# Keeping the inverse transform's exchange in SBUF, with a fixed order of stages and mixed tile widths

## The chip, the cores and the metric

One NeuronCore of a Trainium2 chip. The metric is the device time of one execution in microseconds (us). Engines: PE (TensorE; PEld is its weight load), DVE (VectorE), ACT (ScalarE), POOL (GpSimd), SP (SyncE, which here only issues DMAs). SBUF is the on-chip memory, PSUM the banks that PE writes.

## What is computed

Three stages in a row, on x of 8 x 3072 x 256 in fp32:

```
X = rfft(x, axis=1); y = irfft(X * (filt_r + 1j * filt_i))
logits = y @ w_gate; e = argmax(logits)              # one of 8 experts per token
h = relu(y @ w1[e]); m = gate * sigmoid(y @ w_output_gate)[e] * (h @ w2[e])
out = relu(m @ w_in) ** 2 @ w_out                    # 256 -> 2048 -> 256, 64-bit weights
```

There are 24576 tokens; an expert's inner width is 1024.

## The kernel before

**The Fourier stage** factors the 3072 points as 64 x 48 and runs in four groups (NG, two batch rows each), each through three kinds of step. *A* (12 per group, `steps_a`): DFT over 64 points with the twiddles, four products of 256 columns; one PSUM half is copied by ACT, the other by DVE, and the result is stored to the DRAM scratch `s1` two steps later. *B* (32 per group, two k1 at a time, `b_first`, `b_mid`, `b_second`): loads 192 KB of `s1`, DFT over 48 points (L330 or L334), two copies that swap real and imaginary rows into `q` (L336, L337 on ACT), products with the filter on DVE (L338) and POOL (L339), their sum on DVE (L347), the inverse DFT over 48 points (L355 or L358), a copy by ACT (L360), and a store to the scratch `s2` (L364). Its filter tile serves a pair of steps; `load_f` fills one of four buffers with six DMAs (L231, L239), and `dup_f` (L244) copies it to the upper half of the partitions. *C* (24 per group, two n2 at a time, `c_first`, `c_second`, `c_third`): loads 256 KB of `s2` four steps ahead (L380), the inverse DFT over 64 points (L393) into `yo`, four transposes (L402), a split into two parts, the logits (L416). Every fourth C step starts `route`, which over eight steps finds expert, weight and rank of 1024 tokens, stores the rows to `yd`, and queues eight scatters of token numbers into the lists `tab`; each C step issues at most two of them on POOL (L428).

The reads of `s1` and `s2` turn the order of the indices: that exchange is why they go through DRAM. The factors of the inverse DFT are transposes of the forward ones, made once on chip (`turn_m`).

**Order.** Each engine runs its instructions in program order. The string `order` (L537 to L562) is made by a small planner: at each place it takes the kind that is least far along (B and C offset by 1.2 and 2.4 groups) among those whose inputs have had 4 or 6 steps to reach DRAM. In its result A of one group, B of the one before and C of the one before that alternate; the last group's C steps come alone. The loads for a block's first four steps go out three steps ahead.

**The first layer** begins with `prelude` (about 23 steps, one per place of `order` from two places after the last B step, once three groups are routed; it also waits until those groups' scatters are issued): four tiles of 512 rows (KP) of the leading expert. Then come 40 wide tiles of 512 rows and 15 narrow tiles of 256 (`width`, L743), all of one expert each. Each tile takes eight steps of `up` (L829) and `down` (L845), 96 products in all, and transposes of its rows (L809). Its weights, 2 MB whatever its width, come in quarters: a quarter of the next tile is loaded while the same quarter of this tile runs (L760), and split two quarters later (L789 on ACT, L790 on DVE). `turn_x` writes the split rows with the row index outermost, so an engine's writes step by 16 bytes (L812, L813). The second layer's 64-bit weights are decoded by DVE in small pieces beside the first 35 tiles or so.

**The second layer** reads the results in tiles of 512 rows; `split_t` (L888, L889, L897) reads them with the same 16-byte step.

Of the kernel before, what the change touches and what calls it, by code (L numbers as in the profile page):

```python
# [27 lines left out]
NG = PR  # L28
# [12 lines left out]
NTILE1 = KP + NTILE_T  # L41
NTILE2 = NT // TT
YW = D + 8


def constants():
    """Arrays that depend on the shapes alone: DFT factors with their twiddles, and signs."""
# [8 lines left out]
    # two orders of k2 on the partitions (real 0:24 and 32:56, imaginary 64:88 and 96:120): lower half  # L56
    # first, or upper half first
# [16 lines left out]
    for r in (0, 55, 64, 119):  # L74
# [3 lines left out]
                          e[:, None] == np.arange(E)[None, :]], axis=1)  # L78
    f = np.float32
    return {  # L80
        "ma": np.ascontiguousarray(ma.transpose(1, 0, 2)).astype(f),
        "mb": mb.astype(f),
# [7 lines left out]
def spectral_moe_kernel(ctx: ExitStack, tc: tile.TileContext, x, filt_r, filt_i, w_gate, w_og, w1, w2,  # L90
                        w_in, w_out, c_ma, c_mb, c_mb2, c_sg, c_cum, out, dbg=None):
# [6 lines left out]
    s2 = [dram.tile([96 * N1, PK], F32, name=f"s2_{g}") for g in range(NG)]  # L98
# [7 lines left out]
    # ------------------------------------------------------------ constants on chip  # L106
# [18 lines left out]
    # tables over the 2 E + 1 runs of tiles: TT rows wide by expert, TS rows wide by expert, none left  # L125
# [6 lines left out]
    for i in range(2):  # L132
# [6 lines left out]
    # expert and start of its list  # L139
# [7 lines left out]
    # ------------------------------------------------------------ FFT  # L147
    # pools of stages A and B on the right, those of the last stage on the left
# [11 lines left out]
    NFB = 4  # L160
    fbuf = [fcon.tile([128, 2, KF, D], F32, name=f"fb{i}") for i in range(NFB)]
    map_, xp, aop, bip, qp, yp, bop = (right(fft, n, b) for n, b in (
        ("map", 6), ("xp", 3), ("aop", 3), ("bip", 6), ("qp", 3), ("yp", 3), ("bop", 4)))
# [7 lines left out]
    # gate weights, split, between zeros: (hi | lo) for v = 0, (hi | 0) for v = 1  # L171
    wgs = ccon.tile([128, 2, 2, 224], F32R, name="wgs")
    nc.vector.tensor_copy(wgs, segb[:, 0:1].unsqueeze(2).unsqueeze(3).to_broadcast([128, 2, 2, 224]))
    for v in range(2):
# [3 lines left out]
        ("mip", 6, {}), ("vtp", 6, {}), ("yop", 5, {}), ("ysp", 3, {}), ("rp", 2, {}),  # L178
        ("psA", 3, {"space": PSUM}), ("psL", 1, {"space": PSUM})))
    later = []  # L180
# [8 lines left out]
    # x: partition (r, a), free (j, d)  # L189
# [12 lines left out]
    def load_m(c, i):  # L202
        t = map_.tile([128, 8, 128], F32, name="m")
        nc.sync.dma_start(out=t, in_=c[:, i * 8:(i + 1) * 8, :])
        return t

    ma, mi = {}, {}

    def turn_m(i):
        """the inverse transform's factors: the transposes (1 / S is in mb2)"""  # L210
        t = mip.tile([128, 8, 128], F32, name="m")
        for h in range(2):
            ps = psA.tile([128, 4, 128], F32, name="p")
            for j in range(4):
                nc.tensor.transpose(ps[:, j], ma[i][:, 4 * h + j], ident)
            (nc.scalar.copy if h else nc.vector.tensor_copy)(t[:, 4 * h:4 * h + 4], ps)
        mi[i] = t
# [4 lines left out]
    # pair w of the units (k1 = 2 w + i) and the pair of units 64 - k1 share a filter tile: rows  # L222
    # k1 + 64 a at 0:24, rows 64 (a + 1) - k1 at 32:56; the last tile serves the units 63 and 32
# [24 lines left out]
    ma[0] = load_m(c_ma, 0)  # L248
# [7 lines left out]
    # stage A: DFT over n1, twiddles folded in  # L256
    def steps_a():
        for u in range(len(aunits)):
            g, i = aunits[u]
            if g == 0 and i % 2 == 0 and i // 2 + 1 < 6:  # L260
                ma[i // 2 + 1] = load_m(c_ma, i // 2 + 1)
            if g == 0 and i % 2 == 1:
                turn_m(i // 2)
# [17 lines left out]
    # stage B: DFT over n2, filter, inverse DFT over k2; two k1 at a time  # L281
# [3 lines left out]
    s2v = [s.rearrange("(m k) c -> m k c", k=N1) for s in s2]  # L285
# [56 lines left out]
    def b_mid(u):  # L342
        g, ka, kb, w, up = units[u]
        p, q = pq.pop(u)
        y = yp.tile([128, 512], F32, name="yt")
# [4 lines left out]
    def b_second(u):  # L350
        g, ka, kb, w, up = units[u]
        o = psO.tile([128, 2, D], F32, name="o")
        y = yt.pop(u)
        if not up:
            nc.tensor.matmul(o[0:96].rearrange("p k d -> p (k d)"), mb2[:, up], y)  # L355
        else:
            for k in range(2):
                nc.tensor.matmul(o[0:96, 1 - k], mb2[:, up], y[:, k * D:(k + 1) * D])  # L358
# [18 lines left out]
    def load_v(u):  # L377
        g, j = cunits[u]
# [3 lines left out]
    def c_first(u):  # L382
        g, j = cunits[u]
        if j + AC < UC:
            load_v(u + AC)
# [794 lines left out]
```

## Time and profile before

| | us |
|---|---|
| median of 3 runs (4098.66 to 4108.8) | 4105.96 |
| the profiled execution, its span | 4105.7 |

| busy | PE | DVE | ACT | POOL |
|---|---|---|---|---|
| us | 3841.4 | 2868.0 | 2082.6 | 785.2 |
| share of the span | 94% | 70% | 51% | 19% |

The span of the profiled execution is its own time to the tenth; no time lies around it. A group of instructions has its line, engine, operation, tiles (out<-in), shapes and count, then its busy time in us and the mean ns of one, then the idle time of the engine before it and who ended that. The ends of matmuls are modelled, so the rate of products is read from their starts.

### The profile page before, as it was taken

What the parts mean: (1) busy time and instruction counts of PE and PEld (TensorE: products, weight loads), DVE (VectorE), ACT (ScalarE), POOL (GpSimd) and SP (SyncE); (2) the same over time, 40 slices, a digit from 0 to 9 for tenths busy, and PEclk for the clock granted to TensorE, in tenths of its full rate; (3) what the DMA queues carried; (4) which work ended last, traced back from release to release, by engine and by line L of the source; (5) the groups of instructions that cost most, each with busy time, mean ns of one, the idle gap of its engine ahead of it and who ended that gap; (6) DMA issues with size and microseconds to landing.
All of it is one profiled execution on the core that took longest, in us unless ns stands there. A gap on an engine that the chain in (4) does not pass through costs nothing.

```text
span 4105.7 us, 71680 instructions
## 1 busy us (share of the span) xinstructions
PE 3841.4 (94%) x25828; PEld 3462.9 (84%) x25828; DVE 2868.0 (70%) x5037; ACT 2082.6 (51%) x3875; POOL 785.2 (19%) x743
## 2 busy tenths in 40 slices
PE   6887787699999999999899999999999999999998
PEld 4465555578888888889899999999999999999998
DVE  3555565368888777666677777777777777777775
ACT  3555465235554544455555555555555555555554
POOL 1344564511111111111001001010010110100101
PEclk9998889799999999999999999999999999999999
DMA  9899988334455555458400000000000000000000
GB/s 304 265 241 223 208 189 186 92 114 149 145 151 148 150 150 149 141 146 201 125 27 26 28 22 27 27 24 30 22 27 27 24 26 25 27 27 23 26 22 17
DMA packets 364071, 408.14 MB, mean 99 GB/s; under 512 B 84769, under 2 KB 308738, under 8 KB 360642
## 3 DMA queue, kind: packets, MB, share of 16 engines
q1 hardware_dynamic: 337440, 350.17, 31.2%
q0 software_dynamic: 25248, 53.15, 4.5%
q8 instruction: 203, 3.33, 0.3%
q14 instruction: 154, 1.26, 0.1%
q10 hardware_dynamic: 1026, 0.23, 0.0%
HBM read 271.61 MB, written 131.80 MB: 98 GB/s over the span
## 4 chain that ended last, share of the span: by engine, by line
PE 78%; DMA 8%; DVE 2%; ACT 2%; issue 2%; SPq 1%; POOL 1%; another core or an unknown queue 0%; ACTq 0%; POOLq 0%; DVEq 0%
PE py L957 26%; PE ph L911 16%; PE ph L829 12%; PE py L845 12%; PE px L911 7%; DMA r<-in_moe_w_dram 2%; DMA bi<-s 1%; DMA fb<-in_filt_i_dram 1%; DMA tab<-rowid,si 1%; PE p L393 1%; PE px L809 1%; DMA vt<-s 1%; ACT bh L888 1%; DMA fb<-in_filt_r_dram 1%; PE p L330 1%
## 5 line engine op out<-in xcount | busy, mean ns | idle before, releaser
L957 PE MATMUL py<-woh,hh 128*128 128x256 f32 x3072 | 859.8, 280 | 0.0
L957 PE MATMUL py<-woh,hl 128*128 128x256 f32 x3072 | 857.4, 279 | 0.4 <-DVE hl L944 0.4
L957 PE MATMUL py<-wol,hh 128*128 128x256 f32 x3072 | 854.6, 278 | 0.0
L957 PEld LDWEIGHTS py<-woh,hh 128*128 128x128 f32 x3072 | 578.2, 188 | 0.0
L957 PEld LDWEIGHTS py<-wol,hh 128*128 128x128 f32 x3072 | 578.0, 188 | 0.0
L957 PEld LDWEIGHTS py<-woh,hl 128*128 128x128 f32 x3072 | 576.5, 188 | 0.8 <-DVE hl L944 0.8
L966 POOL DMA_INDIRECT out_dram<-ou,io x192 | 207.9, 1083 | 1904.4 <-ACT C L933 1666.4
L911 PE MATMUL ph<-bh,wsh 128*128 128x256 f32 x1920 | 546.2, 284 | 24.9 <-ACT s L918 18.8
L833 ACT ACTIVATE hh<-ph 128x512 fp32r<-128x512 f32 (+1 forms) x472 | 256.0, 545 | 589.9 <-PE ph L829 498.9
L911 PE MATMUL ph<-bl,wsh 128*128 128x256 f32 x1920 | 539.0, 281 | 0.1
L911 PE MATMUL ph<-bh,wsl 128*128 128x256 f32 x1920 | 537.4, 280 | 0.0
L935 DVE SCALAR_TENSOR_TENSOR q<-C 128x1024 f32<-128x1024 f32 x384 | 468.1, 1219 | 2.3 <-ACT C L933 2.3
L944 DVE TENSOR_TENSOR hl<-q,hh 128x1024 fp32r<-128x1024 f32 x384 | 466.8, 1216 | 1.1 <-ACT hh L942 1.1
L834 DVE SCALAR_TENSOR_TENSOR hl<-ph,hh 128x512 fp32r<-128x512 f32 (+1 forms) x472 | 292.0, 621 | 222.3 <-ACT hh L833 194.7
L929 DVE TENSOR_TENSOR C<-ph,p 128x256 f32<-128x256 f32 x384 | 162.5, 423 | 401.1 <-ACT hh L942 278.2
L942 ACT CAST hh<-q 128x1024 fp32r<-128x1024 f32 x384 | 404.1, 1052 | 1.3 <-DVE q L935 1.3
L933 ACT COPY C<-ph 128x256 f32<-128x256 f32 x384 | 143.2, 373 | 506.6 <-PE ph L911 506.6
L911 PEld LDWEIGHTS ph<-bh,wsh 128*128 128x128 f32 x1920 | 360.9, 188 | 35.4 <-ACT s L918 28.3
L772 POOL DMA_INDIRECT xg<-yd,idx x190 | 200.6, 1056 | 954.1 <-DVE idx L782 906.9
L911 PEld LDWEIGHTS ph<-bl,wsh 128*128 128x128 f32 x1920 | 362.5, 189 | 0.4 <-DVE bl L889 0.4
L911 PEld LDWEIGHTS ph<-bh,wsl 128*128 128x128 f32 x1920 | 361.7, 188 | 0.0
L845 PE MATMUL py<-hh,wh 128*128 128x512 f32 (+1 forms) x944 | 356.9, 378 | 5.1 <-issue 5.1
(271 smaller groups left out, 8679.3 us busy)
## 6 DMA issues: line engine op xcount, KB each, us to landing
r<-in_moe_w_dram SPq DMA_DIRECT2D x448, 256.0 KB
yd<-yo SPq DMA_DIRECT2D x24, 1056.0 KB
xt<-in_x_dram SPq DMA_DIRECT2D x48, 512.0 KB
s<-ao SPq DMA_DIRECT2D x48, 512.0 KB
vt<-s SPq DMA_DIRECT2D x96, 256.0 KB
r<-ytd SPq DMA_DIRECT2D x48, 512.0 KB
bi<-s SPq DMA_DIRECT2D x124, 192.0 KB
s<-bo SPq DMA_DIRECT2D x124, 192.0 KB
```

The source lines that it names most:

```text
L772: nc.gpsimd.indirect_dma_start(out=xg[:, c, :], out_offset=None, in_=yd[0:(NT * GP // NG if t < KP else NT) + 1], in_offset=bass.IndirectO ...
L829: nc.tensor.matmul(ps, a[:, c, f2 * 128:(f2 + 1) * 128], b[:, c, 0:w], start=n == 0, stop=n == 5)
L833: nc.scalar.activation(hh, ps, AF.Relu)
L834: nc.vector.scalar_tensor_tensor(hl, ps, 0.0, hh.bitcast(F32), op0=ALU.max, op1=ALU.subtract)
L845: nc.tensor.matmul(Y[t][h], a[:, f % 2, h * 128:(h + 1) * 128], b, start=f == 0 and i == 0, stop=f == NF - 1 and i == 2)
L911: nc.tensor.matmul(ps, x[:, u, a], y[:, b], start=start and n == 0, stop=n == 2, skip_group_check=True)
L929: nc.vector.tensor_tensor(C[:, 3], V, p5, ALU.add)
L935: nc.vector.scalar_tensor_tensor(q, C, 0.0, C, op0=ALU.max, op1=ALU.mult)
L942: nc.scalar.copy(hh, q)
L944: nc.vector.tensor_tensor(hl, q, hh.bitcast(F32), ALU.subtract)
L957: nc.tensor.matmul(Z[t][k][:, c, :], x[:, 2 * i + k, c * 128:(c + 1) * 128], w[:, 2 * u + i, :], start=u == 0 and m in (0, 6), stop=u == N ...
L966: nc.gpsimd.indirect_dma_start(out=out, out_offset=bass.IndirectOffsetOnAxis(ap=io[:, c:c + 1], axis=0), in_=ou[:, c, :], in_offset=None)
```

## The change

- Stage B's inverse product is turned over: the data `y` are the stationary operand (four products, each 128 weight columns and 96 moving columns), so the result has the 256 channels on the partitions. ACT copies it into `big` (128 x 2 x 96 x 64 fp32, one buffer, 48 KB per partition), two neighbouring floats at a time; `k1_place` makes the two k1 of a step neighbours.
- Stage C no longer loads `s2`: `c_turn` takes 128 x 128 blocks of `big` and turns them back by four PE transposes; the PSUM tile is copied by DVE and ACT in turn. The factors of the inverse DFT come from DRAM (`c_mi`, rows in the order of `k1_place`), 512 KB per four C steps, two buffers. `turn_m`, `s2`, its stores and loads are gone.
- Buffers: filter tiles 4 to 3, `ao` 3 to 2, `q` 3 to 4 (the sum is now written over `q`), `vt` 6 to 2, `yo` 5 to 4, the split 3 to 2, `yt` of the first layer 2 to 1.
- The planner is replaced by a fixed order: B and C of one group follow each other as blocks (35 and 28 steps with their lags), with the A steps of the next group set among them.
- The 512-row tiles hold only full blocks of one expert, so there are 37 of them beside the leading four, and 21 narrow tiles; `slot` spreads the narrow ones among the wide ones. Their places in the results are as before, wide ones first.
- Columns of a wide tile are held by block (`p (c q)`), so `turn_x` and, for the first 41 tiles, `split_t` read and write contiguous runs.

```diff
-NTILE_L = (NT - KP * TT - E * TS) // TT
+NTILE_L = NT // TT - KP - E * (TT - 1) // TT
...
-    NFB = 4
+    NFB = 3
...
+    big = ccon.tile([128, 2, 2 * N2, N1], F32, name="big")
...
     def b_second(u):
-        o = psO.tile([128, 2, D], F32, name="o")
+        o = psO.tile([128, 2, 2 * N2, 2], F32, name="o")
         y = yt.pop(u)
...
-        b = bop.tile([96, 2, D], F32, name="bo")
-        nc.scalar.copy(b, o[0:96])
-
-        def store():
-            for d, at in rows(ka, kb):
-                nc.sync.dma_start(out=s2v[g][:, d, 0:D], in_=b[:, at])
-        later.append(store)
+        for k in range(2):
+            for h in range(2):
+                nc.tensor.matmul(o[:, h, :, 1 - k if up else k], y[:, k * D + h * 128:k * D + (h + 1) * 128], mb2[:, up])
+        at = min(k1_place(ka), k1_place(kb))
+        nc.scalar.copy(big[:, :, :, at:at + 2], o)
...
-    def load_v(u):
+    def c_turn(u):
         g, j = cunits[u]
+        pt = (psP if g < NG - 1 else psA).tile([128, 2, D], F32, name="p")
+        for i in range(2):
+            for h in range(2):
+                n = 2 * j + i
+                nc.tensor.transpose(pt[:, i, h * 128:(h + 1) * 128],
+                                    big[:, h, 2 * n:2 * n + 2].rearrange("p r k -> p (r k)"), ident)
         vt[u] = vtp.tile([128, 2, D], F32, name="vt")
-        nc.sync.dma_start(out=vt[u], in_=s2[g][j * 256:(j + 1) * 256, 0:D].rearrange("(j q) c -> q j c", j=2))
+        (nc.vector.tensor_copy if u % 2 else nc.scalar.copy)(vt[u], pt)
 
     def c_first(u):
-        if j + AC < UC:
-            load_v(u + AC)
+        if j % 4 == 0 and j + 4 < UC:
+            load_m(mi, c_mi, mip, 6 * g + j // 4 + 1)
...
+    LAGC = 4
+
+    def steps_c():
+        for g in range(NG):
+            in_g = lambda u: g * UC <= u < (g + 1) * UC
+            for u in range(g * UC, (g + 1) * UC + LAGC):
+                scatter(2)
+                if in_g(u):
+                    c_turn(u)
+                if in_g(u - 1):
+                    c_first(u - 1)
+                if in_g(u - 4):
+                    c_third(u - 4)
+                if in_g(u - 2):
+                    c_second(u - 2)
+                yield
+
+    order = "a" * UA
     for g in range(NG):
+        next_a = lambda: "a" if g + 1 < NG and order.count("a") < (g + 2) * UA else ""
+        if g == 0:
+            order += "aaaa"
+        ahead.setdefault(len(order) - 3, []).extend(lambda u=g * UB + i: load_b(u) for i in range(AB))
+        for i in range(UB + LAG):
+            order += "b"
+            if i in ((10, 18, 26), (5, 11, 17, 23, 29))[g > 0]:
+                order += next_a()
+        ahead.setdefault(len(order) - 8, []).extend(lambda i=6 * g + i: load_m(mi, c_mi, mip, i) for i in range(1))
+        order += next_a()
+        for i in range(UC + LAGC):
+            order += "c"
+            if i % 3 == 2:
+                order += next_a()
+        order += "--"
...
-    width = [TT if t < KP + NTILE_L else TS for t in range(NTILE1)]
+    NS = NTILE_T - NTILE_L
+    slot, k = [], 0
+    for i in range(NTILE_L):
+        slot.append(i)
+        while (k + 1) * NTILE_L <= (i + 1) * NS:
+            slot.append(NTILE_L + k)
+            k += 1
+    width = [TT] * KP + [TT if i < NTILE_L else TS for i in slot]
...
+        by = "p (c q) -> p c q" if w == TT else "p (q c) -> p c q"
+        hv = xh[:, h, 0:w].rearrange(by, c=n)
+        lv = xl[:, h, 0:w].rearrange(by, c=n)
```

## Rows read from the trace of the kernel before

**Rows 1.** Busy time by stage: stretch, length, busy (instructions), PEclk, DMA share, GB/s.

```profile
0.00:760.00 760.00, 576.26 (x2432) 408.76 (x2432) 413.09 (x908) 382.62 (x720) 330.57 (x314) 0.89 0.88 226
900.00:1600.00 700.00, 700.00 (x3157) 570.46 (x3156) 562.32 (x1103) 350.32 (x491) 123.82 (x122) 1.00 0.51 150
1650.00:1800.00 150.00, 150.00 (x676) 122.21 (x675) 89.51 (x128) 74.50 (x105) 22.15 (x22) 1.00 0.48 135
1817.00:2012.00 195.00, 183.25 (x1491) 179.36 (x1490) 133.05 (x259) 115.66 (x235) 33.19 (x26) 0.99 0.77 197
2015.00:4105.70 2090.70, 2047.82 (x17280) 2036.04 (x17280) 1551.17 (x2352) 1084.84 (x2208) 207.87 (x192) 0.99 0.08 25
```

**Rows 2.** DMA of 0 to 760 us: packets, and the loads of `s2`.

```profile
DMA packets 142715, 171.65 MB, mean 226 GB/s; under 512 B 20882, under 2 KB 128371, under 8 KB 139973
...
vt<-s SPq DMA_DIRECT2D x96, 256.0 KB
```

**Rows 3.** The chain that ended last, Fourier stage: start us, us, what.

```profile
308.17 1.73 PE p L272 x8
...
388.05 4.11 DMA fb<-in_filt_r_dram
...
440.77 10.96 DMA fb<-in_filt_i_dram
```

**Rows 4.** Groups of instructions by line and shape, 0 to 760 us.

```profile
L339 POOL TENSOR_TENSOR q<-q,fb 128x512 f32<-128x512 f32 x128 | 163.7, 1281 | 336.8 <-ACT q L337 120.6 <-DMA s<-ao 77.3 <-DVE fb L244 30.3
L428 POOL DMA_INDIRECT tab<-rowid,si x157 | 160.1, 1020 | 90.6 <-issue 30.2 <-DMA tab<-rowid,si 26.3 <-DVE si L497 16.2
...
L347 DVE SCALAR_TENSOR_TENSOR yt<-q,sg,p 128x512 f32<-128x512 f32 x124 | 92.2, 744 | 3.9 <-POOL q L339 1.8
L338 DVE TENSOR_TENSOR p<-p,fb 128x512 f32<-128x512 f32 x128 | 88.3, 690 | 25.8 <-ACT q L337 24.5 <-PE p L442 0.8
...
L360 ACT COPY bo<-o 96x512 f32<-96x512 f32 x128 | 74.5, 582 | 26.4 <-DMA s<-bo 13.1 <-PE o L355 7.3 <-PE o L358 2.2
...
L336 ACT COPY q<-p 64x512 f32<-64x512 f32 x128 | 73.9, 578 | 133.2 <-PE p L330 68.6 <-PE p L334 49.6 <-issue 5.0
...
L244 DVE COPY fb<-fb 64x1024 f32<-64x1024 f32 x68 | 54.9, 808 | 186.5 <-DMA fb<-in_filt_i_dram 63.5 <-DMA fb<-in_filt_r_dram 42.5 <-DMA s<-bo 35.9
```

**Rows 5.** Groups of instructions by line and shape, 880 to 1795 us.

```profile
L812 ACT CAST xh<-px 128x512 fp32r<-128x512 f32 x80 | 85.7, 1071 | 0.0
...
L850 ACT COPY yt<-py 128x512 f32<-128x512 f32 x78 | 41.9, 594 | 0.0
```

**Rows 6.** Instructions in order of time among the last C steps: start, us, engine.

```profile
690.47 1.13 PE L393 MATMUL p<-vt,m 128*128 128x256 f32 x4 [0.35 <-DVE carry L496]
...
691.81 0.46 PEld L402 LDWEIGHTS p<-ident,yo 128*128 128x128 f32 x4
...
692.24 0.73 PEld L393 LDWEIGHTS p<-vt,m 128*128 128x128 f32 x4
...
707.37 1.13 PE L393 MATMUL p<-vt,m 128*128 128x256 f32 x4 [0.66 <-ACT cn L469]
...
762.93 1.91 PE L393 MATMUL p<-vt,m 128*128 128x256 f32 x4
```

**Rows 7.** Filter loads of L239 on SP: count, ns min/median/max, first and last start.

```profile
L239 SPq DMA_DIRECT2D fb<-in_filt_i_dram x136: 297/356/1653, 23.1 to 647.1; - x136
```

**Rows 8.** The first B product's weight loads, same columns.

```profile
L330 PEld LDWEIGHTS p<-bi,mb x128: 186/190/338, 66.2 to 646.4; 96*128 96x128 f32 x128
```

**Rows 9.** The chain that ended last, the first products of two wide tiles.

```profile
1510.93 1.39 PE py L845 x6
...
1534.01 1.39 PE py L845 x6
```

**Rows 10.** Waits in 1817 to 2012 us: total us, times, longest.

```profile
ACT wh L789 <- DMA r<-in_moe_w_dram: 30.5, 21, 3.5
```

**Rows 11.** Busy time late in the narrow tiles, columns as in rows 1.

```profile
1986.00:1999.00 13.00, 13.00 (x112) 13.00 (x111) 10.06 (x19) 8.19 (x18) 1.62 (x1) 1.00 0.77 208
```

More of the change, by code (lines that the diff above doesn't have):

```diff
@@ L78, in constants @@
                           e[:, None] == np.arange(E)[None, :]], axis=1)
+    rows = np.argsort([k1_place(k) for k in range(N1)])
     f = np.float32
@@ L200, in load_x, with load_m @@
         xt[u] = t
[L202 to L205, printed above, removed]
     ma, mi = {}, {}
[L209 to L217, printed above, removed]
+    def load_m(at, c, pool, i):
+        at[i] = pool.tile([128, 8, 128], F32, name="m")
+        nc.sync.dma_start(out=at[i], in_=c[:, i % 6 * 8:(i % 6 + 1) * 8, :])
     filt = (filt_r, filt_i)
@@ L260, in steps_a @@
             if g == 0 and i % 2 == 0 and i // 2 + 1 < 6:
-                ma[i // 2 + 1] = load_m(c_ma, i // 2 + 1)
-            if g == 0 and i % 2 == 1:
-                turn_m(i // 2)
+                load_m(ma, c_ma, map_, i // 2 + 1)
             if u + 2 < len(aunits):
@@ L507, in steps_b @@
     def steps_b():
[L508 to L516 removed]
+        for g in range(NG):
+            for u in range(g * UB, (g + 1) * UB + LAG):
+                if u < (g + 1) * UB:
+                    b_first(u)
+                if g * UB <= u - 1 < (g + 1) * UB:
+                    b_mid(u - 1)
+                if u - LAG >= g * UB:
+                    b_second(u - LAG)
+                yield
     def advance():
@@ L542, in spectral_moe_kernel @@
-    at = {k: [] for k in "abc"}
-    order = ""
-    def ready(k):
-        n = len(at[k])
-        if n >= NG * size[k]:
-            return False
-        if k == "a":
-            return True
-        b = "ab"["bc".index(k)]
-        m = (n // size[k] + 1) * size[b] + lag[b]
-        return len(at[b]) >= m and at[b][m - 1] + (W0 if n == 0 and k == "b" else WAIT) < len(order)
-    while any(len(at[k]) < NG * size[k] + lag[k] for k in "abc"):
-        best = min((k for k in "abc" if ready(k)), default=None,
-                   key=lambda k: len(at[k]) / size[k] + {"a": 0, "b": 1.2, "c": 2.4}[k])
-        if best is None or 0 <= len(at["b"]) - NG * UB < LAG:
-            best = next((k for k in "abc" if NG * size[k] <= len(at[k]) < NG * size[k] + lag[k]), "-")
-        if best != "-":
-            at[best].append(len(order))
-        order += best
@@ L563, in spectral_moe_kernel @@
-    PF = 3
+        for g in range(NG):
+            in_g = lambda u: g * UC <= u < (g + 1) * UC
[9 more added lines that the diff above has]
+                    c_second(u - 2)
+                yield
+    order = "a" * UA
     ahead = {}
@@ L565, in spectral_moe_kernel @@
     for g in range(NG):
-        ahead.setdefault(at["b"][g * UB] - PF, []).extend(lambda u=g * UB + i: load_b(u) for i in range(AB))
-        ahead.setdefault(at["c"][g * UC] - PF, []).extend(lambda u=g * UC + i: load_v(u) for i in range(AC))
+        next_a = lambda: "a" if g + 1 < NG and order.count("a") < (g + 2) * UA else ""
[6 more added lines that the diff above has]
+                order += next_a()
@@ L884, in split_t @@
         bh, bl = (pl["bp"].tile([128, 7, 256], F32R, name=n) for n in ("bh", "bl"))
-        rv = [[r[:, j].rearrange("p (q c) -> p c q", c=4)[:, 2 * k:2 * k + 2] for k in range(2)] for j in range(2)]
+        by = "p (c q) -> p c q" if t < NWIDE else "p (q c) -> p c q"
+        rv = [[r[:, j].rearrange(by, c=4)[:, 2 * k:2 * k + 2] for k in range(2)] for j in range(2)]
         blk = lambda a: a.rearrange("p (c q) -> p c q", c=2)
```

58 lines of the change are left out of this document (15 added, 43 removed).

## The prediction

> **What bounds the kernel now.** I read the busy time by stage first, since each stage has a limit of its own [rows 1]. The second layer (2015 us to the end) keeps PE busy for 2048 of 2091 us, and the wide tiles of the first layer for all of 900 to 1600 us; neither is limited by anything but TensorE. Two stretches are not. In the Fourier stage, 0 to 760 us, PE, DVE, ACT and POOL are busy 576, 413, 383 and 331 us, the DMA engines 0.88 of the time, and the granted clock averages 0.89. In the narrow tiles, 1817 to 2012 us, PE idles 12 of 195 us.
>
> For the Fourier stage I then read its DMA traffic [rows 2]: 171.65 MB in 142,715 packets, so most packets are 1 KB, and 226 GB/s. The s2 exchange is 96 loads of 256 KB and as many bytes stored: 50 MB, about 49,000 packets of 1 KB. The chain of waits there names loads of the filter tile that took 4.11 to 10.96 us [rows 3]. So transfers hold this stage, and the change takes traffic from them. The question is what limits next.
>
> **Part 1, the exchange.** Busy DMA time is 0.88 x 760 = 669 us, or 4.7 ns a packet. Without s2 231 us of that go; the factors loaded again by each group (4 x 6 x 512 KB in 4 KB packets, about 3,100 packets) cost 15 us by packets or 49 us by bytes. Some 453 to 487 us stay, which no longer fill a stage of 700 us, so engine steps decide. I price one step of each kind.
>
> *A B step.* DVE: 0.69 for L338, 0.744 for L347, and half of 0.808 for the filter copy L244: 1.84 us [rows 4]. ACT: two copies into q, 0.578 each, and the copy out of o, now 384 columns instead of 512. It was 0.582; by columns it would be 0.44. It now writes pairs of floats 256 bytes apart. The nearest row for a scattered write is L812, stride 16 bytes: 1071 against 594 ns for the contiguous L850 [rows 5], so at most 384 x 2.09 ns = 0.80. ACT is 1.60 to 1.96; I take the middle. The Trainium skill (SBUF — State Buffer, in its section on the DMA port swizzle) says that each access that leaves a 16-byte line pays; the trace agrees for L812, and by it, paying on every second element, an estimate is 0.62, which changes no sum here because DVE leads. PE: the first product is half of an A step's four products of 256 columns (1.73 us [rows 3]), 0.87. The second becomes four products with 128 weight columns and 96 moving ones, each two passes. Four single-pass transposes of 128 columns follow each other in 0.43 us (691.81 to 692.24 [rows 6]), 0.107 each; eight such passes are 0.86 if the weight load sets the pace, 0.64 if the 96 columns do. I take 0.86, in place of 0.87 now: no gain. The Trainium skill (TensorE: Matmul & The Clock Gate, LDWEIGHTS) puts a weight load at columns / 1.2 ns whatever the moving side has, 107 ns here; the row agrees, and this rule speaks against narrow moving operands: by it the products cost 0.86, by the streamed columns 0.64, and over 128 steps the two differ by 28 us of PE time, though not of a step that DVE leads.
>
> So the floor of a B step is DVE's 1.84. One loop is longer. With three filter buffers instead of four, the load for pair w + 2 goes into the buffer that the previous step's POOL product still reads. From that step's first product: ACT 1.16, POOL 1.28 and hand-overs, 2.65 us; six issues on SP at 0.36 and a little between, some 2.4 [rows 7]; landing L; copy 0.81; less 1.2 because the product four steps on needs it only after its own matmul. Four steps must cover 4.66 + L, so a step is at least 1.17 + L / 4. L was 4.11 to 10.96 on the old queue; with DMA share near 0.75 I take the short end, 4.6, hence **2.3 us**. Bounds: 1.84 and, at 10.96, 3.9.
>
> *A C step.* Where C steps ran alone, seven took 707.37 - 690.47 = 16.9 us, 2.41 each with their routing [rows 6]. The change adds four transposes (0.43 on PE) and an eviction shared by ACT and DVE. I take 2.41 + 0.43 = **2.84**; below, 2.41 if the transposes fill idle PE time; above, 3.5 if a whole 0.69 eviction lands on the chain as well. Removing the vt load hides nothing else.
>
> *A steps* inside other blocks: PE 1.73 among C steps, which PE limits; about 1.0 among B steps, where an eviction like L338's 0.69 falls on DVE. *Changing blocks:* B's last step drains through 0.87, 1.16, 1.28, 0.74, 0.86, 0.6, and C fills through 0.43, 0.6, 0.87, 0.6, 0.43, 0.6: 9 us per group, which the old mixed order covered.
>
> *Queues.* SP loses 128 stores and 96 loads, gains 24 loads. The scatters (two per C step, 1.02 us each plus 0.3 between, L428 [rows 4]) now crowd on POOL: 2.6 of 2.84 us. A backlog would hold the next block's POOL product; no scatter is issued in B steps, and I book nothing because four C steps in each block issue none, with a bound of 5 us per group. Two ao buffers instead of three in the opening: 4 us (0 to 8). Dropping the 48 transposes of turn_m gains nothing there, as the opening waits for transfers. The smaller vt, yo and yt pools cost nothing as long as their cover holds: vt is filled a step ahead by PE; a yo tile lives some 18 C steps counting its store's landing, against 16 that four buffers give when that store is late, so up to 2 steps in each chunk of four are at stake, 24 x 5.7 us at worst, and none if SP issues the store as soon as its route is done, which its queue, lightened by 220 transfers, allows; yt's store has a whole tile to land.
>
> Sum to the last C product: opening 66 (the first B product now starts at 66.2 [rows 8]) + 4; B 128 x 2.3 = 294; C 96 x 2.84 = 273; A steps 13 x 1.0 + 19 x 1.73 = 46; four block changes 36: **719 us**. It now ends at 762.93 + 1.91 = 764.8 [rows 6]. Gain 46 us. The first layer starts right behind, as now: its prelude takes some 23 steps and starts with the last C block, which has 28.
>
> **Part 2, narrow tiles among wide.** A wide tile takes 1534.01 - 1510.93 = 23.08 us [rows 9], a narrow one 195 / 15 = 13.0 [rows 1], and over the 15 ACT waits 30.5 us for weights [rows 10]. The last 13 us without such a wait hold 112 products and transposes [rows 11], 0.116 each; a narrow tile has 100, so 11.6 us at PE's pace. Before: 44 x 23.08 + 195 = 1210.5. After, 41 wide and 21 narrow at 11.6: 1190, 20 less. But DVE is 8.9 us per narrow tile, and the decoding of the second layer's weights adds (562.3 / 700 - 89.5 / 150) x 23.08 = 4.8 us per tile [rows 1], 13.7 in all against 11.6. Decoding covers the first 34 tiles or so, about 11 of them narrow: 0 to 23 us back, I take 12. Net **-8** (-20 to +3).
>
> **Part 3, blocked columns.** xh and xl go from 1.07 to about 0.6 us on engines that wait for PE anyway: nothing, except at the head of the second layer, where the splits stand alone: -1.5.
>
> The profiled execution took 4105.7 us, the median is 4105.96, so no correction: 4105.7 - 46 - 8 - 1.5 = **4050**.
>
> **Rivals.** *The steps reach their floors* (B 1.84, C 2.41, part 2 full): 128 x 0.46 + 96 x 0.43 + 12 = 112 us more, 3938. For it: DMA share falls far below 0.88. Against: nothing in [rows 2] or the page shows B steps at one engine's floor. Halfway is 3994. Chance 0.14.
>
> *The clock takes half.* The mean grant is 0.89 [rows 1], which is 22% of the time at the lower of its two levels, 1.2 GHz. In a B step PE then needs 2 x 1.73 = 3.5 us, 1.2 over the step; over 22% of the B steps that is 34 us, over 40%, 61. That gives 4084 to 4111: little or no change. Chance 0.2. For it: B blocks now stand alone and PE is the only engine with a slower level. Against: C blocks become dense.
>
> *The filter buffer holds B.* If L stays at 7.5, midway in the old range, a step is 3.0 and the time 4050 + 128 x 0.7 = 4140, slower than before. It decides against the change from L = 6.5 (step 2.8). For it: loads of 24 rows queue behind x and s1 transfers and six issues share SP with the rest. Against: 30% less traffic. Chance 0.15.
>
> *It does not do what it says* (transfers still at 0.88, engines waiting as now): part 2 alone is left, 4095. Chance 0.03.
>
> **Numbers.** The forecast, 4005 to 4080, has the remaining 0.48. Faster by over 0.3% (12 us, about what a measurement tells from no change) means under 4093.6: 0.48 + 0.14 + 0.08 of the clock case = 0.70; within: the rest of it, 0.12, and the last rival, 0.15; slower: the filter case, 0.15. The range leaves out the lowest part of the floor case and the worst of the filter case: 3975 to 4125.
>
> **What would show it.** Right: no transfers of s2, DMA share under 0.75 up to 720 us; first B product near 70; B products 2.2 to 2.5 us apart in the last group's B block and C products 2.7 to 3.0 apart; last C product near 719; 0.86 us for the four products of L355's successor; the copy into big between 0.44 and 0.80; no weight waits in the first layer, ending some 55 us earlier than 2012. Wrong: waits of L244 for filter loads over 2 us in each pair, a granted clock below 0.85 in B blocks, POOL products late behind scatters, or narrow tiles at 13 us or more with PE behind hl.

## The result and the profile after

The changed kernel takes **4048.9 us** (median of 4 runs, 4045.9 to 4062.6) against 4103.65 (4098.66 to 4108.8) for the kernel before on the same chip: ratio 0.9866, 95% interval 0.9842 to 0.9891. The prediction said 4050, faster. The number came out right by luck, because most of its terms are not: on this chip the stage that was to give 46 us gave 10, and a part costed at 1.5 us gave 31, the most of all.

One thing is needed to read the figures below. The chips differ: two of them ran the kernel before in 4104 and 4107 us, the three that ran all experiments but the last in 4137 (4136.6 to 4136.9). Each ratio is to the kernel before on the same chip; experiments are compared with the changed kernel as c0_after ran it on a chip of the second kind. A profile shows one run, for c0_after the slowest of its four (4049.8 us, median 4039.4) and for e5 and e7 the fastest (4024.7 and 4007.9), so differences between two profiles carry some 10 us that the medians do not have.

Busy time by stage of the changed kernel, columns as in [rows 1]:

```profile
0.00:760.00 760.00, 645.62 (x3477) 516.54 (x3477) 448.39 (x974) 400.87 (x771) 340.87 (x332) 0.89 0.65 178
900.00:1600.00 700.00, 690.49 (x3693) 585.57 (x3692) 562.89 (x1205) 349.25 (x584) 119.51 (x118) 1.00 0.59 165
1650.00:1800.00 150.00, 150.00 (x817) 128.80 (x816) 91.61 (x153) 76.24 (x128) 29.47 (x26) 1.00 0.55 159
1990.00:4048.00 2058.00, 2033.86 (x17280) 2029.29 (x17280) 1499.44 (x2352) 1052.88 (x2208) 207.99 (x192) 1.00 0.08 25
```

The DMA share of the Fourier stage fell from 0.88 to 0.65, as the change promises. The DMA view of the same 760 us answers to [rows 2]; no load of `s2` is left in it:

```profile
DMA packets 94101, 135.01 MB, mean 178 GB/s; under 512 B 18113, under 2 KB 76450, under 8 KB 91346
```

Three lines by shape, 0 to 800 us, answer to [rows 4]. The copy into `big` took 0.493 us, between the bounds 0.44 and 0.80, and waits for filter loads fell from 106 us to 26:

```profile
L354 ACT COPY big<-o 128x384 f32<-128x384 f32 x128 | 63.1, 493 | 29.4 <-PE o L352 21.2 <-issue 5.7
L243 DVE COPY fb<-fb 64x1024 f32<-64x1024 f32 x68 | 49.3, 725 | 27.8 <-DMA fb<-in_filt_i_dram 15.1 <-DMA fb<-in_filt_r_dram 10.7 <-issue 0.2
L335 POOL TENSOR_TENSOR q<-q,fb 128x512 f32<-128x512 f32 x128 | 164.0, 1283 | 204.7 <-ACT q L333 169.6 <-DMA fb<-in_filt_i_dram 9.7 <-DMA fb<-in_filt_r_dram 8.0
```

So transfers hold this stage far less than before. Yet its last C product starts at 753.7 us instead of 764.2, where 719 was forecast. These are all C products, before and then after (ns min/median/max, first and last start):

```profile
L393 PE MATMUL p<-vt,m x384: 377/379/797, 202.0 to 764.2; 128*128 128x256 f32 x192
L389 PE MATMUL p<-vt,m x384: 379/379/634, 157.7 to 753.7; 128*128 128x256 f32 x192
```

From the traces, by stage (starts of products):

| us | before | after | predicted change | measured change |
|---|---|---|---|---|
| first B product | 66.6 | 66.1 | +4 | 0 |
| last C product | 764.2 | 753.7 | -46 | -10 |
| from there to the end of the first layer | 1248.3 | 1232.2 | -8 | -16 |
| from there to the end (second layer) | 2093.2 | 2062.4 | -1.5 | -31 |

### The profile page after: what moved, and what is told of

Read it like the earlier page. It is cut to its first block, busy times and chain, and to the rows that moved or that the text cites. A ratio compares the mean times of both kernels' runs of the same rounds, so it can differ in the third digit from the quotient of the medians.

```text
span 4048.3 us, 74500 instructions
## 1 busy us (share of the span) xinstructions
PE 3881.3 (96%) x27092; PEld 3562.3 (88%) x27092; DVE 2817.7 (70%) x5126; ACT 2040.8 (50%) x3965; POOL 776.2 (19%) x743
## 3 DMA queue, kind: packets, MB, share of 16 engines
q1 hardware_dynamic: 297600, 318.71, 27.6%
## 4 chain that ended last, share of the span: by engine, by line
PE 78%; DVE 2%; ACT 1%; DMA 1%; issue 1%; another core or an unknown queue 0%; SPq 0%; POOL 0%; POOLq 0%; ACTq 0%; DVEq 0%
PE py L958 26%; PE ph L912 17%; PE ph L829 13%; PE py L845 12%; PE px L912 7%; PE px L807 1%; DVE wl L788 1%; PE p L389 1%; DVE hl L834 0%; DMA raw<-in_moe_w_in_dram 0%; PE o L352 0%; PE p L398 0%; DMA out_dram<-ou,io 0%; PE lt L412 0%
## 5 line engine op out<-in xcount | busy, mean ns | idle before, releaser
L912 PEld LDWEIGHTS ph<-bh,wsh 128*128 128x128 f32 x1920 | 360.1, 188 | 12.4 <-ACT bh L889 5.1
L845 PE MATMUL py<-hh,wh 128*128 128x512 f32 (+1 forms) x992 | 365.0, 368 | 0.0
L829 PE MATMUL ph<-xh,wh 128*128 128x512 f32 (+1 forms) x992 | 356.5, 359 | 7.6 <-DVE hl L834 6.9
```

The costliest lines, as they stand in the source:

```text
L829: nc.tensor.matmul(ps, a[:, c, f2 * 128:(f2 + 1) * 128], b[:, c, 0:w], start=n == 0, stop=n == 5)
L845: nc.tensor.matmul(Y[t][h], a[:, f % 2, h * 128:(h + 1) * 128], b, start=f == 0 and i == 0, stop=f == NF - 1 and i == 2)
L912: nc.tensor.matmul(ps, x[:, u, a], y[:, b], start=start and n == 0, stop=n == 2, skip_group_check=True)
```

## The experiments

### Which part gives what: e1, e2, e3

e1 takes part 3 out: `turn_x` and `split_t` keep the 16-byte step of the kernel before.

```diff
-        by = "p (c q) -> p c q" if w == TT else "p (q c) -> p c q"
+        by = "p (q c) -> p c q"
...
-        by = "p (c q) -> p c q" if t < NWIDE else "p (q c) -> p c q"
+        by = "p (q c) -> p c q"
```

> The changed kernel with the columns of wide tiles held as before, so that the splits of both layers step by 16 bytes again. Prediction: the blocked columns are worth 1.5 us, all at the head of the second layer, so about 4050. Theory from the two traces: each tile of the second layer began with a wait of PE for ACT, which the 0.65 us copies of the split delayed; the second layer took 2091 us before and 2062 after, so it should take about 2090 again, the total 4075 to 4085, with the waits of the up product for ACT's first copy back at 47 us. Rival: the 28 us come from another place (the second layer's start, its stores), and then the second layer stays at 2062 to 2066. The first layer should lose 0 to 10 us, since DVE is short of time in its narrow tiles.

Measured: 4074.1 us (4068.8 to 4082.7), ratio 0.9848 (0.9815 to 0.9882); the second layer takes 2093.8 us, as before the change, against 2064.8 in c0_after. What went is seen in the waits of PE in the second layer (us in total, times, longest). The kernel before:

```profile
PEld ph L911 <- ACT s L918: 28.3, 47, 0.8
PE ph L911 <- ACT s L918: 18.8, 47, 0.6
```

The changed kernel:

```profile
PEld ph L912 <- ACT s L919: 4.0, 7, 0.6
PE ph L912 <- ACT s L919: 2.6, 7, 0.4
```

And e1:

```profile
PEld ph L912 <- ACT s L919: 26.8, 47, 0.6
PE ph L912 <- ACT s L919: 17.4, 47, 0.4
```

There are 48 tiles, so the wait stood at every change of tile. ACT in order of time at one of them, in the kernel before, shows what is late:

```profile
2173.84 1.79 ACT L888 CAST bh<-r 128x256 fp32r<-128x256 f32 x3
2175.52 0.38 ACT L918 COPY s<-ph 128x256 f32<-128x256 f32 x1
```

Three casts of the next tile's rows stand ahead of the copy `s` that PE needs. With single floats 16 bytes apart one takes 668 ns, contiguous 446 ns (the kernel before, then the changed one):

```profile
L888 ACT CAST bh<-r 128x256 fp32r<-128x256 f32 x144 | 85.9, 668 | 3.8 <-DMA idsc<-idx 3.8
```

```profile
L889 ACT CAST bh<-r 128x256 fp32r<-128x256 f32 x144 | 54.5, 446 | 4.0 <-DMA idsc<-idx 4.0
```

The wait rows show 19 us of the 31; the pace shows all of it. In the same 200 us in the middle of the layer, the kernel before and the changed one (columns as in [rows 1]):

```profile
2100.00:2300.00 200.00, 198.26 (x1683) 197.46 (x1682) 148.58 (x224) 104.48 (x216) 21.01 (x19) 1.00 0.08 24
```

```profile
2100.00:2300.00 200.00, 200.00 (x1707) 199.91 (x1706) 147.54 (x235) 103.04 (x218) 16.86 (x16) 1.00 0.08 25
```

24 products more in 200 us are 1.4%, or 29 us over the layer, at the same granted clock.

e2 keeps the changed kernel's tiles but puts the narrow ones last; e3 keeps part 1 alone (the old widths, order and column layout).

```diff
+    slot = list(range(NTILE_T))
```

> The changed kernel with its 21 narrow tiles after the 37 wide ones. Prediction: mixing is worth 8 us net (20 at best, less what DVE loses while it decodes), so 4056. Theory from the traces: in the changed kernel PE is idle only some 10 us among the mixed tiles, and 21 narrow ones in a row would cost 13.0 us each instead of 11.6 to 12.2, so 18 to 29 us more, 4066 to 4078, with waits of the weight split for its load of some 40 us in the narrow tiles. Rival: DVE's crowding takes back all that mixing gives, and the total stays within 5 us of 4048.

```diff
-NTILE_L = NT // TT - KP - E * (TT - 1) // TT
+NTILE_L = (NT - KP * TT - E * TS) // TT
...
+    slot = list(range(NTILE_T))
...
+        by = "p (q c) -> p c q"
```

> Only the Fourier stage of the change; both layers' tiles, their number, order and columns as before. Prediction: 46 us less than before, 4060. Theory from the traces: the last C product ended 10 us earlier and the first layer began 30 us earlier, so 10 to 30 us less than before, 4076 to 4096, with the second layer at 2090 again and the last C product near 754. Rival: the stage gains nothing by itself (less than 5 us).

Measured: e2 4060.4 us (ratio 0.9817, 0.9787 to 0.9848), e3 4068.3 (0.9838, 0.9806 to 0.987). From the last C product to the end of the first layer, e2 takes 1249.1 us and c0_after 1231.5: mixing the same tiles is worth 17.6 us (21 in the medians). But e3, with the old 44 wide and 15 narrow tiles, the narrow ones last, takes 1236.3, and e1, with the new tiles mixed and the old layout, 1234.6. The new cut has six narrow tiles more and three wide ones less; it takes back nearly all that mixing brings. Such times have some play: in the profiles that leave the first layer as it is in the changed kernel (c0_after, e4, e5, e6, e10, e11, e12) it takes 1220.6 to 1233.2 us. On chips of this kind part 1 alone gives 69 us (4136.9 to 4068.3), part 3 another 35 (4074.1 to 4039.4), and part 2 nothing that the runs can tell (4068.3 to 4074.1, ranges overlapping). The parts were not taken one by one on a chip of the first kind, where all together give 55 us instead of 97.

### What holds a B step: e4, e10, e6

The prediction had a loop through three filter buffers. e4 gives a fourth; e10 does the same on top of e5 (below).

```diff
-    NFB = 3
+    NFB = 4
```

> The changed kernel with four filter buffers instead of three. Prediction: the loop through the filter buffer sets the B step at 2.3 us, above the floor of 1.84; then a fourth buffer should bring B steps to 1.84 to 2.0 and the total down by 35 to 55 us. Theory from the trace: DVE and POOL waited only some 45 us for filter loads in 128 steps, and the waits for the copy out of o and for ACT are longer, so B steps stay at 2.1 or more and the total falls by less than 15 us.

> e5 with four filter buffers instead of three. If the loop through three filter buffers set the B step, as the prediction had it, B steps fall by 0.2 us or more each and this is 20 us or more faster than e5. If they do not set it (e4 had the same B steps as the first profile), it is within 8 us of e5, by what the first filter loads of a block come earlier.

Measured: e4 4036.6 us (ratio 0.9749, 0.9715 to 0.9783), c0_after's ratio being 0.9758 (0.9739 to 0.9776); e10 4034.0 (0.9743, 0.9717 to 0.9768), e5's being 0.9736. The fourth buffer does nothing that the runs can tell, and the B steps stay: 2.41, 2.73, 2.75 and 2.47 us in e4's four blocks, 2.51, 2.88, 2.78 and 2.39 in c0_after's (from the first product of a block to that of its last step, divided by the 31 steps between). On average that is 2.59 in e4, and 2.53 to 2.64 in c0_after, e1, e2, e3 and e7, whose Fourier stage is the same. The filter loop is not what holds them.

e6 takes one PSUM buffer from `p` and gives it to `o`.

```diff
-    psP = right(fft, "psP", 3, space=PSUM)
-    psO = right(fft, "psO", 1, space=PSUM)
+    psP = right(fft, "psP", 2, space=PSUM)
+    psO = right(fft, "psO", 2, space=PSUM)
```

> Two PSUM buffers for o and two for p, instead of one and three. Theory (in the B block that stands alone, the loop product, copy, product through the one o buffer, 0.9 us of TensorE wait in every second step, holds a step at 1.97 us): steps of the last group's B block fall toward DVE's 1.84, at most 4 us, and up to 15 us over all blocks. Rival (the pipe of two p buffers becomes the limit, since p waits for two ACT copies and a DVE pass): B steps of 2.6 us and more, 15 to 60 us slower.

Measured: 4308.8 us (4304.8 to 4316.2), ratio 1.0407 (1.0387 to 1.0427), 269 us above c0_after; the rival's sign, and far beyond its size. Instructions of e6 in order of time (start, us, engine, what, idle before it):

```profile
606.72 1.10 PE L326 MATMUL p<-bi,mb 96*128 96x512 f32 x2 [2.00 <-issue]
...
607.85 0.58 ACT L332 COPY q<-p 64x512 f32<-64x512 f32 x1 [2.23 <-PE p L326]
608.44 0.58 ACT L333 COPY q<-p 64x512 f32<-64x512 f32 x1
...
609.05 0.70 DVE L334 TENSOR_TENSOR p<-p,fb 128x512 f32<-128x512 f32 x1 [2.44 <-ACT q L333]
...
609.66 0.74 DVE L343 SCALAR_TENSOR_TENSOR q<-q,sg,p 128x512 f32<-128x512 f32 x1
...
610.81 1.10 PE L330 MATMUL p<-bi,mb 96*128 96x256 f32 x4 [2.13 <-DVE q L343]
```

The order on DVE closes a loop: L343 of step u, which frees p(u), stands behind L334 of step u + 1, which waits for both ACT copies of p(u + 1). With two buffers the first product of u + 2 waits for p(u). One turn is the product, 1.10, two copies, 1.17, L334, 0.70, L343, 0.74, and hand-overs: 610.81 - 606.72 = 4.09 us, and each turn is one step. The changed kernel has three buffers, and two steps in each turn. Its DVE alone, in the last group's B block:

```profile
608.26 0.70 DVE L334 TENSOR_TENSOR p<-p,fb 128x512 f32<-128x512 f32 x1 [1.27 <-ACT q L333]
608.99 0.75 DVE L343 SCALAR_TENSOR_TENSOR q<-q,sg,p 128x512 f32<-128x512 f32 x1
610.02 0.70 DVE L334 TENSOR_TENSOR p<-p,fb 128x512 f32<-128x512 f32 x1 [0.28 <-ACT q L333]
610.63 0.74 DVE L343 SCALAR_TENSOR_TENSOR q<-q,sg,p 128x512 f32<-128x512 f32 x1
611.40 0.69 DVE L243 COPY fb<-fb 64x1024 f32<-64x1024 f32 x1
612.21 0.70 DVE L334 TENSOR_TENSOR p<-p,fb 128x512 f32<-128x512 f32 x1
```

612.21 - 608.26 = 3.95 us for two steps, 1.98 each: about the same turn. So `p` is a limit that binds at once when a buffer goes. The steps of the whole stage fit this: between the starts of the inverse products (L352) of two steps that both run at the full clock the median is 3.96 us in e6, 1.98 in the changed kernel, and 1.99 in c0_after, e3 and e4. DVE's 1.84 lies just below, so a fourth buffer could bring little by itself; it was not tried. The Trainium skill (Perfetto Trace Analysis, Identifying Performance Opportunities) says that the same gap coming back on the engine that should be saturated can mean too few buffers for the next tile; here the trace agrees, with 2.00 and 2.13 us of idle PE ahead of the two products above and, over whole B blocks, steps that go from 2.4-2.9 to 4.7-5.1 us. Part of that is the clock: where e6's steps run at the lower of its two levels they take 4.90 us, and in its B blocks the granted clock is 0.50 to 0.70, in c0_after's 0.81 to 0.88.

### What the changes of block cost: e5, e11, e12

In the changed kernel 18.5, 15.9 and 21.3 us pass between the last transposes of a C block and the first product of the next B block. PE in order of time at the first of these, the last `c_turn` and the first B product:

```profile
219.04 0.60 PE L373 MATMUL p<-ident,big 128*128 128x128 f32 x4
...
237.58 3.78 PE L326 MATMUL p<-bi,mb 96*128 96x512 f32 x4 [4.47 <-DMA bi<-s]
```

e5 puts the first four B steps among the last four C steps and issues their loads five C steps earlier.

```diff
-        ahead.setdefault(len(order) - 3, []).extend(lambda u=g * UB + i: load_b(u) for i in range(AB))
-        for i in range(UB + LAG):
+        if g == 0:
+            ahead.setdefault(len(order) - 3, []).extend(lambda u=g * UB + i: load_b(u) for i in range(AB))
+        for i in range(4 if g else 0, UB + LAG):
...
-        order += "--"
+            if g + 1 < NG:
+                if i == UC - 5:
+                    ahead.setdefault(len(order), []).extend(lambda u=(g + 1) * UB + i: load_b(u) for i in range(AB))
+                if i >= UC:
+                    order += "b"
+        if g + 1 == NG:
+            order += "--"
```

> The changed kernel itself again, on the chip of the next runs. Theory: what the first profile showed repeats: B steps of 2.0 to 2.6 us, C steps of 2.7 to 2.9, and between the last block of a C stage and the first product of the next B block 16 to 21 us. Last C product 740 to 754 us, first layer ends 1232 us (within 4) after that, second layer 2062 (within 3). If the last group's C block (3.7 us a step in the first profile) was a chance collision, it is near 3.0 here; if it belongs to the kernel, it is 3.5 or more again.

> The first four B steps of groups 1 to 3 stand among the last four (draining) C steps of the group before, and their loads are issued five C steps earlier; nothing else moves. Theory (the changes between blocks cost about 25 us a group, most of it in C to B, because the B pipe fills only when C has drained and its loads start late): C to B falls from 16-21 us to about 6-10, three times: 25 to 40 us less to the last C product, and 25 to 40 us less in all. Rival (DMA sets the stage: what is saved at a change comes back as waits for bi and fb in the B block): less than 10 us, with longer B steps.

Measured: c0_after 4039.4 us (4037.3 to 4049.8), ratio 0.9758; e5 4029.6 (4024.7 to 4030.0), ratio 0.9736 (0.9718 to 0.9754), 10 us less. The same two lines of e5:

```profile
216.71 0.60 PE L373 MATMUL p<-ident,big 128*128 128x128 f32 x4
...
221.81 1.02 PE L326 MATMUL p<-bi,mb 96*128 96x512 f32 x2
```

The gap is 5.1 us, and by the first and last products of the blocks the three gaps together are 29 us shorter than in c0_after. But of the B blocks behind them two are 9 and 12 us longer (89.7 and 82.6 us from the first to the last product of L326 against 81.0 and 70.6), and the last C product comes only 14 us earlier. Even these 14 us are not shown to be e5's: e3 and e7, whose Fourier stage is c0_after's, have it at 735.3 and 737.6 us, as early as e5. What stands is the 10 us in the medians, and e12 against e11 (below), the same edit again, gives 10 us too. Both readings were half right.

What the early steps run into is on POOL, whose first products come 12.4, 13.5 and 15.2 us after PE's in e5. POOL in order of time in c0_after, where the same is seen and PE's first B product of this block starts at 235.12:

```profile
237.57 0.95 POOL L424 DMA_INDIRECT tab<-rowid,si  x1 [4.12 <-DMA tab<-rowid,si]
...
243.37 0.95 POOL L424 DMA_INDIRECT tab<-rowid,si  x1 [0.68 <-DMA tab<-rowid,si]
248.82 0.95 POOL L424 DMA_INDIRECT tab<-rowid,si  x1 [4.50 <-DMA tab<-rowid,si]
...
251.06 3.71 POOL L335 TENSOR_TENSOR q<-q,fb 128x512 f32<-128x512 f32 x3
```

The scatters go into four tables in turn, so each waits for the landing of the one four before it (6.6 us in the median here, up to 9.7), and POOL's first product comes 16 us after PE's. PE then stands still:

```profile
253.29 2.07 PE L326 MATMUL p<-bi,mb 96*128 96x512 f32 x2 [11.92 <-DVE q L343]
```

The same happens ahead of the other two blocks (430.4 after 415.8, 604.5 after 593.4). e11 moves scatters out of the C blocks into the B blocks that follow, with two buffers more for the token numbers `si`; e12 is e5 and e11 together.

```diff
-        si = rp.tile([128, TC], I32, name="si", bufs=4)
+        si = rp.tile([128, TC], I32, name="si", bufs=6)
...
+                if g and u >= g * UB + 4 and u % 3 and (g + 1 < NG or len(scat) > 20):
+                    scatter(1)
...
-                scatter(2)
+                scatter(1 if g + 1 < NG else 2)
```

> The scatters of the routing are spread: one per C step instead of two in the first three groups, and the rest two in every three B steps of the next group (the last B block leaves the same 20 to the last C block as before). Theory (in c0_after GpSimd works off a backlog of scatters, each waiting up to 4.5 us for the landing of the one four before it into the same table, and reaches its first product of the B block 11 to 15 us after TensorE's first one, in three groups; PE and ACT stand behind it): the first GpSimd product follows within 4 us, the waits of the scatters for a table fall from 118 us to under 50, and the last C product comes 20 to 35 us earlier than in c0_after; time 20 to 35 us below it (ratio 0.967 to 0.971). Rival (the backlog is covered, since B has to wait for its loads at the start anyway): under 8 us.

> e5 and e11 together. Theory: e5 gave back in the B blocks what it won at the changes because its early B steps stood behind the scatters; with these gone the two add up, 40 to 55 us below c0_after (ratio 0.962 to 0.966). Rival (both take away the same wait at the change of blocks): the same as e11 within 8 us.

Measured: e11 4071.4 us (4070.1 to 4075.3), ratio 0.9844 (0.9823 to 0.9866), 32 us slower than c0_after; e12 4061.0 (0.9817, 0.9795 to 0.9838). Both forecasts fell. POOL in e11, where PE's first product starts at 231.4:

```profile
234.72 1.26 POOL L335 TENSOR_TENSOR q<-q,fb 128x512 f32<-128x512 f32 x1 [10.28 <-ACT q L333]
...
243.27 1.26 POOL L335 TENSOR_TENSOR q<-q,fb 128x512 f32<-128x512 f32 x1 [3.33 <-DVE fb L243]
247.94 1.27 POOL L335 TENSOR_TENSOR q<-q,fb 128x512 f32<-128x512 f32 x1 [3.41 <-issue]
249.37 1.01 POOL L424 DMA_INDIRECT tab<-rowid,si  x1 [0.16 <-DVE q L343]
```

The first product does come 3.3 us after PE's, and the scatters wait 70 us for tables instead of 118. But the block is 93 us long instead of 84 (L326), the last C product comes at 781.1 us, 29 us later than in c0_after, and DVE's waits for filter loads in 66 to 760 us rise from 33 to 78 us: a scatter, 1.01 us and 0.3 between, now stands beside two of three POOL products of 1.27. That is 2.6 us in such a step and 2.1 on average, in steps of 2.4 to 2.9, so POOL has little slack, and by these waits the filter buffers that its products read come free late. The backlog's stall is real; spreading it over the B steps costs more than it frees. A cheaper way, more tables or smaller stores beside the scatters, was not tried.

### What decoding costs the narrow tiles: e7

The second layer's weights are decoded on DVE in all tiles of the first layer; e7 does it in the wide ones alone.

```diff
-        if f not in (1, 5) and dec:
+        if f not in (1, 5) and dec and width[t] == TT:
```

> Weights of the second layer are decoded in the wide tiles alone, no longer in the narrow ones. Theory (the prediction's: VectorE has 13.7 us of work in an 11.6 us narrow tile while it decodes, 12 us in all): the first layer after the last C product takes 1220 to 1227 us instead of 1231.5. Rival (TensorE idles only some 10 us in the whole mixed stretch, so VectorE's queue hides nearly all of it): 1229 to 1233, no change in the time. If the decoding then ends too late, the head of the second layer grows from its 2064.8.

Measured: 4015.9 us (4007.9 to 4023.3), ratio 0.9713 (0.969 to 0.9735), 24 us below c0_after; from the last C product the first layer takes 1205.3 us instead of 1231.5, twice the theory's estimate and 15 us below the lowest of the unchanged ones (1220.6). Windows of c0_after:

```profile
900.00:1200.00 300.00, 290.23 (x1558) 245.44 (x1556) 242.66 (x549) 148.53 (x249) 49.21 (x52) 0.99 0.60 161
1200.00:1500.00 300.00, 297.52 (x1570) 251.49 (x1569) 249.65 (x528) 148.19 (x247) 48.84 (x49) 1.00 0.62 168
```

The same of e7:

```profile
900.00:1200.00 300.00, 300.00 (x1587) 255.66 (x1587) 232.25 (x480) 152.65 (x254) 55.20 (x48) 1.00 0.59 163
1200.00:1500.00 300.00, 300.00 (x1631) 257.80 (x1630) 230.45 (x464) 153.19 (x256) 59.80 (x52) 1.00 0.60 166
```

PE idles 12 us in these 600 in c0_after and not at all in e7, and e7 does 3218 products and transposes there instead of 3128, 2.9% more. The idle time alone does not show that, since a product that follows a stall counts as busy. In c0_after decoding itself waits, too, and VectorE's queue with it (900 to 1600 us, c0_after and then e7):

```profile
DVE ea L646 <- DMA raw<-in_moe_w_in_dram: 17.1, 4, 5.4
```

```profile
DVE ea L646 <- DMA raw<-in_moe_w_in_dram: 4.3, 2, 2.4
```

The second layer starts no later for it (2063.3 us long).

### A faster version: e9

e5 and e7 together.

> e5 (first four B steps among the draining C steps) and e7 (decoding in wide tiles alone) together; scatters as in the changed kernel. Theory (the two work in different stages and add up): e7's 23.6 us and e5's 9.9 us below c0_after's 4039.4, so 4006 us, ratio 0.967 to 0.970; last C product 8 to 20 us before that of c0_after, first layer 1202 to 1208 us after it, second layer 2062 to 2066. Rival (a Fourier stage that ends earlier only makes the first layer wait for its gates and gathers): the same as e7 alone, 4016 (ratio 0.971).

Measured: 4025.8 us (4023.2 to 4031.0), ratio **0.9800 (0.9786 to 0.9813)**, on a chip of the first kind, where the changed kernel has 0.9866 (0.9842 to 0.9891): faster than both kernels, by 23 us in the medians than the changed one. The forecast was a ratio of 0.967 to 0.970, from chips of the second kind, so it neither met this nor can be tested by it; e7 alone was not run on a chip of the first kind, so what e5 adds to it there is not shown. The second layer takes 2063.4 us; the first, from the last C product, 1214.0 instead of 1232.2. The last C product is at 751.9: of the Fourier stage's gain nothing is left there. The last group's C block starts at 659.9, only 3 us earlier than in the changed kernel (663.1), and takes 86.3 us. It takes 84.9 in the changed kernel's profile on the first kind of chip and 67 to 72 in the seven profiles of c0_after, e1 to e5, and e7 on the second kind, where the prelude of the first layer runs beside it as well. Why it takes longer on the first kind is open.

## Why the prediction was right in sum and wrong in its parts

The sum met the measured time by luck. The Fourier stage was given 36 us too much, the second layer 29 and the first 8 too little, and these errors cancel.

**The exchange** was to save 46 us to the last C product and saved 10 in the profile. By the starts of products in the changed kernel:

- *B blocks.* 302.5 us over the four blocks, from the first product of each to that of its last step; predicted 124 x 2.3 + 13 A steps = 298. The size was right by luck and the cause wrong: the step "one loop is longer", through the filter buffers, does not hold (e4, e10). I had not counted the three buffers of `p`, whose turn (e6) gives 1.98 us, the median step at the full clock. Against that the sum left out the lower clock level: 18 of the 128 steps run at it, and such a step takes 3.42 us (below), some 26 us in all by an estimate of 18 x (3.42 - 1.98). The A steps and the starts of the blocks have the rest. The granted clock is 0.85 to 0.90 in these blocks.
- *C steps.* Without the A steps among them (4, 6 and 6 at 1.73 us) the first three blocks run at 2.42, 2.37 and 2.39 us, against 2.84 predicted: the four transposes and their eviction cost nothing, the lower bound. The last block, at 3.68 in this profile (3.05 in c0_after's), takes back 19 of the 31 us so gained.
- *Changing blocks* was the term that failed. Nine us per group were priced as one drain and one fill; the seven changes take 46 us from B to C and 56 from C to B, some 43 more than the 36 booked for them and the 23 that the A, B and C steps among them cost at the predicted prices. The routing's tail, loads of `bi` that start late (4.47 us above) and the scatters lie there. The scatters I had seen, bounded at 5 us per group and booked at nothing; they cost PE up to 11.9 us in one stall in c0_after, while in this profile POOL's first products come 3 to 8 us behind PE's.
- *The opening, the smaller pools and the queues* cost nothing, as said: the first B product is at 66.1 us.

The inverse products of four B steps of the last group, and the granted clock (the last figure but two) beside the first and the last of them:

```profile
600.01 1.86 PE L352 MATMUL o<-mb,q 128*128 128x96 f32 x8
603.43 1.86 PE L352 MATMUL o<-mb,q 128*128 128x96 f32 x8
...
608.79 1.13 PE L352 MATMUL o<-mb,q 128*128 128x96 f32 x8
...
610.76 1.03 PE L352 MATMUL o<-mb,q 128*128 128x96 f32 x8
```

```profile
599.00:602.00 3.00, 3.00 (x12) 2.73 (x12) 2.97 (x11) 1.25 (x3) 0.40 (x1) 0.50 0.70 226
610.50:612.00 1.50, 1.50 (x11) 1.29 (x11) 1.47 (x3) 0.99 (x3) 0.84 (x1) 1.00 0.39 84
```

**Narrow among wide** was to give 8 us. Mixing gives 17.6 over the same tiles in a row, but decoding takes back 26 (e7) instead of the 12 that I took, outside the range of 0 to 23. What is left of part 2 is e1 against e3: 1.7 us less in the first layer and 6 us more in the medians, neither clear of the play. Of the 16 us by which the first layer is shorter, 12 belong to part 1, as far as profiles on two kinds of chip can tell: e3 has them with the old tiles (1236.3 against 1248.3). That fits the first product of the layer, which now stands 11 to 16 us before the last C product instead of 4 behind it.

**Blocked columns** were costed at 1.5 us with the words "engines that wait for PE anyway". They gave 31. The page has PE busy for all but 43 us of the second layer [rows 1], and I took that for the end of the matter; the view of waits would have shown 47 of them, one per tile, on the engine that bounds the stage.

**The copy into `big`**: 0.493 us for 384 columns is 1.28 ns a column, against 2.09 for `xh` at 16-byte steps [rows 5]. The Trainium skill's rule on 16-byte lines (SBUF — State Buffer, in its section on the DMA port swizzle) made an estimate of 0.62. By the measurement, pairs of floats 256 bytes apart cost only 0.05 us over the 0.44 by columns. The estimate used half of the rule: the same sentence asks for at least two hits per line for full bandwidth, which pairs have and single floats have not. The casts of part 3 agree with it, `xh` falling from 1071 to 586 ns.

**The rivals.** The clock took no half, 0.89 over the stage before and after, but its lower level costs the B blocks some 26 us, near the 34 that this rival named. The filter loads were not late: DVE waited 26 us for them in all. The steps reached a floor in C and not in B. The price of the last rival was a slip, 4105.7 - 8 being 4098 and not 4095; it changes no chance.

## What to carry to other kernels

A wait that comes once in every tile on the engine that bounds the stage is money, however short: multiply it by its count before costing an edit at nothing. To find what holds a pipelined step, go round every ring of buffers, PSUM's too, and count how many steps share one turn of it. When mixed stages become blocks, price each change of block from the in-order queues: what is still queued on each engine when the next block's first instruction comes.

## What the hardware showed beside that

The same 297,600 packets of the main queue took 27.6% of 16 engines' span on the first chip and 29.5% on c0_after's: 1117 and 1194 us. The kernel before, at a DMA share of 0.88, differs by 33 us between such chips, but it was profiled on one of them only, so no trace shows where. The changed kernel has its last C product at 753.7 and 751.7 us on the two, which is chance: in c0_after the four B blocks are 25 us longer (327.1 us against 302.5), the three changes from C to B 12 us shorter, and the last C block 14 us shorter. In the Fourier stage the granted clock is 0.99 to 1.00 in the dense C blocks of the first three groups, 0.81 to 0.88 in c0_after's B blocks and 0.50 to 0.70 in e6's, where PE waits in every step. A B step of the changed kernel takes 1.98 us at the full clock in the median and 3.42 at the lower level.
